# Another seven-product form for attention plus FFN: four products share a PSUM bank that is read in between

## The chip, the core and the metric

The kernel runs on one core of a Trainium2 chip. The metric is the device time of one execution in microseconds (us). "The kernel before" is the version without the change, "the kernel after" the one with it. Engines go by the profile's names: PE is TensorE's matmuls and PEld its weight loads, DVE is VectorE, ACT is ScalarE, POOL is GpSimd, SP is SyncE.

## The reference

`q`, `k` and `v` are 8 x 12 x 448 x 64 (batch, heads, sequence, head size) in float32. The attention's output goes, as 3584 tokens of 768, through a feed-forward network with SiLU:

```python
scores = np.matmul(q, k.transpose(0, 1, 3, 2)) / np.sqrt(64)
attn = softmax(scores)                      # over the keys
x = np.matmul(attn, v)                      # -> (8 * 448) x (12 * 64)
h = x @ w_in                                # 768 x 2048
g = h * (1.0 / (1.0 + np.exp(-h)))
out = g @ w_out                             # 2048 x 768
```

## The kernel before

**Attention.** A unit is one batch and one group of four heads; batch 0 is cut into two pieces of 224 queries, so that there are 27 units, numbered 0 to 26 in order of batch (units 11 and 12, 13 and 14, 25 and 26 are three of the pairs below). For each unit, q and k come by DMA and are transposed on VectorE (`turn_q` L323, `turn_k` L305), TensorE makes scores (L336), ScalarE takes their exponents (`expo` L373) and TensorE multiplies these by v (`attend` L399, L415). Units 0 to 6 are worked on one by one; from unit 7 on two work as a pair: their last, half-filled key rows share one 128-row matmul. The attention of a pair has three parts: part 0 makes the sums of the exponents (L415), parts 1 and 2 make the two halves of the output, each for both units, in 32 column-tiled matmuls of 128x32 weights (24 of full rows and 8 of half rows). VectorE adds exponents up first (`add_e` L384), inverts the sums (`inverse`) and scales each half into `xT` (`norm` L482), which holds half of x, transposed, in fp16.

**First matmul.** For batches 0 to 5, `ffn1` (L496) makes h in blocks of 128 features by 448 tokens, six matmuls each, into one PSUM bank; ScalarE takes the tanh (L507) and VectorE makes (tanh + 1) * h (`gate` L543), which is the SiLU, into `G` (or `X` for one token tile in each four batches). Batches 6 and 7 (`PB` = 6) use another form: for each of eight values of f, `pair_product` (L632) makes a 2 x 2 block product (two batches by two 128-feature blocks, f and f + 8, over two halves of 768) with seven products of three matmuls instead of eight. The sums that it needs are made by VectorE beforehand: of tokens, `combine_x` (L590), and of weights, `combine_w_in` (L608). Copies and adds (`pair_copy` L657, `pair_add` L663) put the products together, and ScalarE takes the SiLU itself (`silu` L670), for which it loads another function table (`first_silu` L667).

**Second matmul.** Tokens go in 28 tiles of 128. A quad is two token tiles by two column halves of 384, over two halves of 2048. Quad 0 is computed plainly (`plain` L718). For quads 1 to 13 `product` (L704) makes seven products of eight matmuls of 384 columns instead of eight, by Strassen's form: products 3 and 5 add up in one PSUM bank, 4 and 2 in another, 1 and 7 in a third, and 6 has a bank of its own. `combine_g` (L694) makes the five sums of gates that this needs, in two halves each, three of them in buffers `S` and two in place; `combine_w` makes five sums of weights once. `take_3` and the others (L766 to L780) read the banks: three copies on ScalarE and four adds on VectorE, and two more adds on VectorE between buffers in SBUF (`less_12`, `less_21`). Each of the four output blocks goes from an `ost` buffer to memory in four DMAs, most of them issued by SyncE (`store` L762). The quads 11 and 13 (`FAR`) keep their outputs in old `xT` buffers. Since a pair of batches has seven tiles, quad 3 takes its first tile from batch 1 and its second from batch 2.

**The order.** All engines' instruction orders are written out by hand, in a plan that is computed when the kernel is built. `Order` holds a free time for each engine; an `Op` has an estimated duration, the operations that it waits for, and a bias that ranks it among those that are ready. `Ring` models a set of buffers: `m_ring` the four single PSUM banks (attention, h, products and plain products), `s_ring` the two two-bank tiles of scores, `sg_ring` the three `S` buffers, `ost_ring` the output buffers, and others the rest. TensorE's next work is chosen among scores, attention and the list `moe`: the first of its first 24 entries whose operands are ready by the plan, and for which a bank and the buffers that it names are free. An entry may be ready before the one ahead of it, so quads, `ffn1` blocks and f-pairs mix. VectorE and ScalarE take the ready operation of least time plus bias. As the plan's order is the program's order, an operation that isn't ready in time on the chip holds up everything behind it on its engine. A block of `ffn1` of a new pair of batches also waits for the products that read the part of `G` that it overwrites; the list of these products stands in `queue_ffn1`, and for the f-pairs in `free`.

## Time and profile before

| what | before |
|---|---|
| device time, median of 3 runs (range) | 396.12 us (396.03 to 396.42) |
| span of the profiled execution, first to last instruction | 394.4 us |
| mean granted clock of TensorE in it | 0.998 |
| PE busy | 386.5 us, 98%, 3679 matmuls |
| DVE busy | 311.3 us, 79%, 653 instructions |
| ACT busy | 243.2 us, 62%, 378 instructions |
| POOL busy | 83.6 us, 21%, 153 instructions |

The span and all rows of the profile come from one execution; its own time is the span and what lies around the program, and the median is 1.7 us above the span. A row of groups gives the line, the engine, the operation, the tiles written and read, the number of instructions, their busy time and the mean of one in ns, and then the idle time just before them with what ended most of it. Matmuls overlap each other in the pipeline: a row's duration is not the distance at which they follow. A row of the timeline gives the start, the time from the start of its first instruction to the end of its last, the instructions, and in brackets how long the engine stood idle before it and who ended that. A row of the chain of waits gives the start and the length of a stretch on the path to the last instruction.

### The profile page before, as it was taken

What the parts mean: (1) busy time and instruction counts of PE and PEld (TensorE: products, weight loads), DVE (VectorE), ACT (ScalarE), POOL (GpSimd) and SP (SyncE); (2) the same over time, 40 slices, a digit from 0 to 9 for tenths busy, and PEclk for the clock granted to TensorE, in tenths of its full rate; (3) what the DMA queues carried; (4) which work ended last, traced back from release to release, by engine and by line L of the source; (5) the groups of instructions that cost most, each with busy time, mean ns of one, the idle gap of its engine ahead of it and who ended that gap; (6) DMA issues with size and microseconds to landing.
All of it is one profiled execution on the core that took longest, in us unless ns stands there. A gap on an engine that the chain in (4) does not pass through costs nothing.

```text
span 394.4 us, 9273 instructions
## 1 busy us (share of the span) xinstructions
PE 386.5 (98%) x3679; PEld 199.0 (50%) x3679; DVE 311.3 (79%) x653; ACT 243.2 (62%) x378; POOL 83.6 (21%) x153
## 2 busy tenths in 40 slices
PE   7999999999999999999999999999999999999995
PEld 6667764443444444554444444344444555556663
DVE  2466676999999697896888786988879898787863
ACT  4988885696863868626868429686593227872110
POOL 6632546315004242500051221120000000000000
PEclk9999999999999999999999999999999999999999
DMA  7999999919034863582145751531100131001334
GB/s 113 205 210 210 166 179 164 175 36 141 1 76 88 142 95 47 75 158 71 25 49 81 139 109 46 71 48 42 42 1 2 40 87 35 2 1 42 80 82 121
DMA packets 35356, 34.44 MB, mean 87 GB/s; under 512 B 11376, under 2 KB 33776, under 8 KB 35312
## 3 DMA queue, kind: packets, MB, share of 16 engines
q0 software_dynamic: 24784, 22.82, 39.2%
q1 hardware_dynamic: 9952, 10.33, 9.6%
q10 hardware_dynamic: 576, 0.69, 0.6%
q8 instruction: 29, 0.48, 0.5%
q14 instruction: 15, 0.12, 0.1%
HBM read 45.61 MB, written 11.01 MB: 144 GB/s over the span
## 4 chain that ended last, share of the span: by engine, by line
PE 94%; DMA 3%; DVE 1%; ACT 1%; POOL 0%; issue 0%; POOLq 0%
PE p L704 29%; PE h L496 29%; PE s L336 12%; PE a L399 10%; PE f L632 8%; PE o L718 3%; DMA rq<-in_q_dram 3%; PE a L415 2%; PE z L1491 1%; ACT E L373 0%; DVE S L694 0%; POOL rk L249 0%; DVE rq L323 0%; DVE rdn L466 0%; DVE ost L766 0%
## 5 line engine op out<-in xcount | busy, mean ns | idle before, releaser
L373 ACT ACTIVATE E<-s 128x896 f16<-128x896 f32 (+1 forms) x172 | 150.0, 915 | 48.6 <-PE s L336 47.5
L496 PE MATMUL h<-xT,w_in_t 128*128 128x448 f16 (+1 forms) x672 | 118.6, 327 | 0.0
L496 PEld LDWEIGHTS <-w_in_t 128*128 128x128 f16 x672 | 61.2, 98 | 54.0 <-issue 18.0
L507 ACT ACTIVATE th<-h 128x448 f16<-128x448 f32 (+1 forms) x112 | 54.3, 495 | 31.4 <-PE h L496 22.5
L543 DVE SCALAR_TENSOR_TENSOR G<-th,h 128x448 f16<-128x448 f16 (+2 forms) x112 | 55.1, 507 | 15.3 <-ACT th L507 13.3
L270 POOL DMA_DIRECT2D V<-in_v_dram x88 | 48.5, 568 | 56.5 <-PE a L399 42.7
L336 PE MATMUL s<-rq,KT 32*128 32x448 f16 (+4 forms) x768 | 50.9, 337 | 1.4 <-DVE rq L323 0.9
L704 PEld LDWEIGHTS <-G 128*128 128x128 f16 x384 | 36.5, 98 | 28.1 <-issue 4.4
L704 PEld LDWEIGHTS <-S 128*128 128x128 f16 x312 | 29.3, 98 | 23.9 <-issue 5.2
L399 PE MATMUL a<-E,V 128*32 128x448 f16 (+3 forms) x864 | 40.4, 335 | 0.0
L255 POOL DMA_DIRECT2D rq<-in_q_dram x27 | 15.1, 560 | 113.0 <-PE s L336 82.9
L704 PE MATMUL p<-D,G 128*128 128x384 f16 x208 | 37.6, 326 | 0.0
L704 PE MATMUL p<-w_out_t,S 128*128 128x384 f16 x208 | 37.2, 326 | 0.1
L482 DVE SCALAR_TENSOR_TENSOR xT<-a,rdn 128x448 f16<-128x448 f32 (+1 forms) x54 | 28.7, 565 | 7.4 <-PE a L399 6.5
L336 PEld LDWEIGHTS <-KT 32*128 32x128 f16 (+2 forms) x864 | 17.5, 98 | 29.6 <-issue 25.9
L704 PE MATMUL p<-w_out_t,G 128*128 128x384 f16 x176 | 31.9, 326 | 0.0
L399 PEld LDWEIGHTS <-V 128*32 128x32 f16 (+2 forms) x864 | 18.2, 95 | 22.4 <-issue 14.7
L384 DVE TENSOR_TENSOR T<-T,E 128x1792 f16<-128x1792 f16 x20 | 21.8, 1089 | 8.0 <-ACT E L373 7.9
L694 DVE TENSOR_TENSOR S<-G 128x512 f16<-128x512 f16 x70 | 25.3, 414 | 3.2 <-PE p L704 3.0
L384 DVE TENSOR_TENSOR T<-E,E 128x1792 f16<-128x1792 f16 x20 | 21.6, 1082 | 5.6 <-ACT E L373 5.6
L776 ACT COPY ost<-p 128x384 f32<-128x384 f32 x13 | 6.2, 480 | 27.4 <-PE p L704 22.6
L305 DVE STREAM_TRANSPOSE KT<-rk 128x256 f32<-128x256 f32 (+3 forms) x48 | 16.6, 384 | 7.0 <-DMA rk<-in_k_dram 6.2
(74 smaller groups left out, 370.2 us busy)
## 6 DMA issues: line engine op xcount, KB each, us to landing
out_dram<-ost SPq DMA_DIRECT2D x194, 48.0 KB, 1.7
rk<-in_k_dram POOLq DMA_DIRECT2D x24, 224.0 KB, 5.9
rq<-in_q_dram POOLq DMA_DIRECT2D x21, 224.0 KB, 5.2
w_in_t<-in_moe_w_in_dram POOLq DMA_DIRECT2D x6, 512.0 KB, 11.2
w_out_t<-in_moe_w_out_dram POOLq DMA_DIRECT2D x4, 768.0 KB, 13.5
V<-in_v_dram POOLq DMA_DIRECT2D x43, 64.0 KB, 3.9
V<-in_v_dram POOLq DMA_DIRECT2D x40, 48.0 KB, 4.0
out_dram<-ost SPq DMA_DIRECT2D x8, 96.0 KB, 2.2
```

Of the source, the lines that this page charges most:

```text
L270: nc.gpsimd.dma_start(out=VT[b][32 * x : 32 * (x + 1), hs, 0:count, :], in_=v[b, hs].rearrange("h (i g) d -> i h g d", g=TPP)[:, :, first ...
L336: nc.tensor.matmul(out=pS[p0 : p0 + 32 * (x1 - x0), h % 2, at : at + nq], lhsT=KT[(b, hg)][32 * h : 32 * (h + 1), c, x0:x1, :, e], rhs=QT[ ...
L373: nc.scalar.activation(out=E[(n, w)][0:kr, 2 * y : 2 * y + 2, 0:nk], in_=pS_t[(n, w, y)][0:kr, :, 0:nk], func=AF.Exp, scale=attn_scale,)
L384: nc.vector.tensor_tensor(out=T[n], in0=T[n] if step else E[(n, 0)], in1=E[(n, step + 1)], op=ALU.add,)
L399: nc.tensor.matmul(out=a[32 * h : 32 * (h + 1), 0:nq], lhsT=w, rhs=e[k0:k1, h, at : at + nq], start=start, stop=stop,)
L482: nc.vector.scalar_tensor_tensor(out=x3(b, cc)[:, cc % 3, 32 * g0 : 32 * g1], in0=acc[(n, part)][:, 0:nq], scalar=0.5, in1=rdn_t[n].rearra ...
L496: nc.tensor.matmul(out=h[:, 0 : t1 - t0], lhsT=w_in_t[:, cc, 128 * f : 128 * (f + 1)], rhs=x3(b, cc)[:, cc % 3, t0:t1], start=(cc == 0), s ...
L507: nc.scalar.activation(out=th, in_=h_t[(b, f, t0)][:, 0 : t1 - t0], func=AF.Tanh)
L543: nc.vector.scalar_tensor_tensor(out=dst[:, f, at + lo : at + hi], in0=th_t[(b, f, t0)][:, lo - t0 : hi - t0], scalar=1.0, in1=h_t[(b, f, ...
L632: nc.tensor.matmul(out=pp_t[(f, PBANK[m])], lhsT=w[:, c, :], rhs=a[:, c, :], start=(c == 0 and m in (1, 6, 5, 7)), stop=(c == 2), skip_gro ...
L694: nc.vector.tensor_tensor(out=dst[:, f0:f1], in0=x[:, f0:f1], in1=y[:, f0:f1], op=op)
L704: nc.tensor.matmul(out=pr_t[(qd, BANK[m])][:, 0:OH], lhsT=w[:, f, :], rhs=W_[m][:, f, :], start=(f == 0 and BANK[m] == m), stop=(f == HF - 1),
```

## The change

The change replaces the seven products in both places by another set of seven. For a quad with token tiles a and b, feature halves 0 and 1, gates Ga0 to Gb1 and weight blocks B00 to B11:

- S5 = Gb0 + Gb1, S6 = S5 - Ga0, S7 = Ga0 - Gb0, S3 = Ga1 - S6 (four sums of gates, S7 in place);
- W5 = B01 - B00, W6 = B11 - W5, W4 = B10 - W6, W7 = B11 - B01 (four sums of weights, W7 in place);
- P1 = Ga0 B00, P2 = Ga1 B10, P3 = S3 B11, P4 = Gb1 W4, P5 = S5 W5, P6 = S6 W6, P7 = S7 W7;
- the outputs are P1 + P2, P1 + P6 + P5 + P3, P1 + P6 + P7 + P4 and P1 + P6 + P7 + P5.

P1, P6, P7 and P4 add up in one bank, which is read after P1 (ScalarE copies it to the output block 00), after P1 + P6 (ScalarE, to 01), after P1 + P6 + P7 (VectorE adds it to 11) and after all four (ScalarE, to 10). P2 has a bank, which VectorE adds to 00. P5 and P3 share a third: ScalarE copies P5 to 11, and VectorE adds P5 + P3 to 01. So a quad has four copies on ScalarE and three adds on VectorE, all into the output buffers; the buffers `tmp` are gone, and there are seven `ost` buffers instead of four. The products stand in `moe` as 1, 5, 6, 2, 7, 3, 4, an `S` buffer is taken for one sum at a time instead of three at once, and the list of products that hold `G` is 1, 2, 3, 4, 7.

The f-pairs get the same form: bank A (products 1, 6, 7, 4) is one half of a two-bank score tile, of which the other half isn't used, and B (2) and C (5, 3) are single banks. A pair has three copies on ScalarE and three adds on VectorE, into SBUF buffers "p", "q" and "u", and four SiLUs, three from these and one from the bank. Before, it had two copies, five adds and four SiLUs. What `combine_x` and `combine_w_in` make is unchanged.

```diff
     NE, NX3, NT_ = 9, 6, 2
     NXT = 3 * NX3
-    NSG, NTMP, NOST = 3, 3, 4
+    NSG, NOST = 3, 7
     attn_scale = 1.0 / (D**0.5)
 
...
@@ -514,24 +514,23 @@
     HF = NFF // 2
     G = const.tile([128, NFF, 2 * S], FP16, name="G")
     X = const.tile([128, NFF, 128], FP16, name="X")
-    W_ = {m: const.tile([128, HF, OH], FP16, name=f"D{m}") for m in (1, 4, 6)}
+    W_ = {m: const.tile([128, HF, OH], FP16, name=f"D{m}") for m in (4, 5, 6)}
     B_ = {
         (i, j): w_out_t[:, HF * i : HF * (i + 1), OH * j : OH * (j + 1)]
         for i in range(2)
...
+    W_[1], W_[2], W_[3], W_[7] = B_[0, 0], B_[1, 0], B_[1, 1], B_[0, 1]
...
     def combine_w(m, f0, f1):
-        i0, i1, op = {
-            1: ((0, 0), (1, 1), ALU.add),
-            4: ((1, 0), (0, 0), ALU.subtract),
-            6: ((0, 0), (0, 1), ALU.add),
-            3: ((0, 1), (1, 1), ALU.subtract),
-            7: ((1, 0), (1, 1), ALU.add),
+        x, y = {
+            5: (B_[0, 1], B_[0, 0]),
+            6: (B_[1, 1], W_[5]),
+            4: (B_[1, 0], W_[6]),
+            7: (B_[1, 1], B_[0, 1]),
         }[m]
         nc.vector.tensor_tensor(
-            out=W_[m][:, f0:f1], in0=B_[i0][:, f0:f1], in1=B_[i1][:, f0:f1], op=op
+            out=W_[m][:, f0:f1], in0=x[:, f0:f1], in1=y[:, f0:f1], op=ALU.subtract
         )
 
     def gate(b, f, t0, t1):
...
-    PBANK = {1: "A", 2: "A", 6: "B", 5: "C", 3: "C", 7: "D", 4: "D"}
+    PBANK = {1: "A", 6: "A", 7: "A", 4: "A", 2: "B", 5: "C", 3: "C"}
 
     def pair_product(f, m):
-        if m in (1, 5):
-            pp_t[(f, PBANK[m])] = ps.tile(
-                [128, 512], FP32, name=f"f_{f}_{m}", tag="m", bufs=4
-            )[:, 0:S]
-        elif m == 6:
-            two = ps.tile([128, 2, 512], FP32, name=f"f_{f}_{m}", tag="s", bufs=2)
-            pp_t[(f, "B")], pp_t[(f, "D")] = two[:, 0, 0:S], two[:, 1, 0:S]
+        if m in (2, 5):
+            t = ps.tile([128, 512], FP32, name=f"f_{f}_{m}", tag="m", bufs=4)
+            pp_t[(f, PBANK[m])] = t[:, 0:S]
+        elif m == 1:
+            t = ps.tile([128, 2, 512], FP32, name=f"f_{f}_{m}", tag="s", bufs=2)
+            pp_t[(f, "A")] = t[:, 0, 0:S]
         x = {(r, i): x3(PB + r, 3 * i) for r in range(2) for i in range(2)}
         lo, at = f // 4 * 4, slice(128 * (f % 4), 128 * (f % 4 + 1))
         a, w = {
...
@@ -643,24 +641,19 @@
             "p": ("rq", NRQ, [128, TPP * D], FP16),
             "q": ("rk", NRK, [128, TPP * D], FP16),
             "u": ("KT", 3, [128, NCH, 4, 32, 2], FP16),
-            "v": ("T", NT_, [128, HG, S], FP16),
         }[name]
         t = sb.tile(shape, dt, name=f"{name}_{f}", tag=tag, bufs=n)
...
         return pf_t[(f, name)]
 
...
         nc.scalar.copy(out=pair_tmp(f, name), in_=pp_t[(f, at)])
 
-    def pair_add(f, to, x, y):
-        x = pp_t[(f, x)] if x in "BCD" else pf_t[(f, x)]
-        y = pf_t[(f, y)]
-        out = pf_t[(f, to)] if (f, to) in pf_t else pair_tmp(f, to)
-        nc.vector.tensor_tensor(out=out, in0=x, in1=y, op=ALU.add)
+    def pair_add(f, to, x):
+        t = pf_t[(f, to)]
+        nc.vector.tensor_tensor(out=t, in0=pp_t[(f, x)], in1=t, op=ALU.add)
 
     def first_silu():
         t = const.tile([128, 1], FP16, name="first_silu")
...
     def combine_g(qd, m, f0, f1):
         a, b = 2 * qd, 2 * qd + 1
+        if m != 7 and (qd, m) not in S_t:
+            S_t[(qd, m)] = sb.tile([128, HF, 128], FP16, name=f"S_{qd}_{m}", tag="S", bufs=NSG)
         x, y, op = {
-            5: (rows(a, 0), rows(a, 1), ALU.add),
-            2: (rows(b, 0), rows(b, 1), ALU.add),
-            1: (rows(a, 0), rows(b, 1), ALU.add),
-            6: (rows(b, 0), rows(a, 0), ALU.subtract),
-            7: (rows(a, 1), rows(b, 1), ALU.subtract),
+            5: (rows(b, 0), rows(b, 1), ALU.add),
+            6: (S_t.get((qd, 5)), rows(a, 0), ALU.subtract),
+            7: (rows(a, 0), rows(b, 0), ALU.subtract),
+            3: (rows(a, 1), S_t.get((qd, 6)), ALU.subtract),
         }[m]
-        if m > 5:
-            dst = x
-        else:
-            if (qd, m) not in S_t:
-                S_t[(qd, m)] = sb.tile([128, HF, 128], FP16, name=f"S_{qd}_{m}", tag="S", bufs=NSG)
-            dst = S_t[(qd, m)]
+        dst = rows(b, 0) if m == 7 else S_t[(qd, m)]
         nc.vector.tensor_tensor(out=dst[:, f0:f1], in0=x[:, f0:f1], in1=y[:, f0:f1], op=op)
 
-    BANK = {3: 3, 5: 3, 4: 4, 2: 4, 1: 1, 7: 1, 6: 6}
+    BANK = {1: 1, 6: 1, 7: 1, 4: 1, 2: 2, 5: 5, 3: 5}
 
     def product(qd, m):
-        w = {3: rows(2 * qd, 0), 4: rows(2 * qd + 1, 1), 6: rows(2 * qd + 1, 0), 7: rows(2 * qd, 1)}
+        w = {1: rows(2 * qd, 0), 2: rows(2 * qd, 1), 4: rows(2 * qd + 1, 1), 7: rows(2 * qd + 1, 0)}
         w = w[m] if m in w else S_t[(qd, m)]
         if BANK[m] == m:
             pr_t[(qd, m)] = ps.tile([128, 512], FP32, name=f"p_{qd}_{m}", tag="m", bufs=4)
@@ -730,10 +719,6 @@
 
     def bank(qd, m):
         return pr_t[(qd, m)][:, 0:OH]
-
-    def tmp(qd, name):
...
@@ -762,40 +747,18 @@
             eng.dma_start(out=dst, in_=ost_t[(qd, i, j)][32 * w : 32 * (w + n), :])
             w, turn = w + n, turn + 1
 
...
+    OUT = {1: (0, 0), 5: (1, 1), 6: (0, 1), 4: (1, 0)}
+    SUM = {2: (0, 0), 7: (1, 1), 3: (0, 1)}
+
+    def take_copy(qd, m):
+        nc.scalar.copy(out=ost(qd, *OUT[m]), in_=bank(qd, BANK[m]))
+        if m == 4:
+            store(qd, *OUT[m])
+
+    def take_sum(qd, m):
+        t = ost_t[(qd, *SUM[m])]
+        nc.vector.tensor_tensor(out=t, in0=bank(qd, BANK[m]), in1=t, op=ALU.add)
+        store(qd, *SUM[m])
 
...
@@ -950,7 +913,7 @@
                         made += (
                             [plain_op.get(x) for x in ((0, 0), (0, 1), (1, 0), (1, 1))]
                             if qd == 0
-                            else [pr_op.get((qd, m)) for m in (3, 4, 6, 7)]
+                            else [pr_op.get((qd, m)) for m in (1, 2, 3, 4, 7)]
                         )
                 return made
 
...
-                    read("v", "DVE", lambda: pair_add(f, "v", "D", "u"), [op, done["u"]])
                 elif m == 5:
...
                 elif m == 2:
-                    gate_of(0, 0, "A", [op], m_ring.give)
+                    read("11", "DVE", lambda: pair_add(f, "p", "B"), [op, done["p"]], m_ring.give)
+                    gate_of(0, 0, "p", [done["11"]], rq_ring.give)
+                elif m == 7:
+                    read("22", "DVE", lambda: pair_add(f, "q", "A"), [op, done["q"]])
+                    gate_of(1, 1, "q", [done["22"]], rk_ring.give)
                 elif m == 3:
-                    read("12", "DVE", lambda: pair_add(f, "p", "C", "u"), [op, done["u"]], m_ring.give)
-                    gate_of(1, 0, "p", [done["12"]], rq_ring.give)
+                    read("12", "DVE", lambda: pair_add(f, "u", "C"), [op, done["u"]], m_ring.give)
+                    gate_of(1, 0, "u", [done["12"]], kt_ring.give)
                 else:
-                    read("21", "DVE", lambda: pair_add(f, "u", "D", "u"), [op, done["12"]], s_ring.give)
-                    gate_of(0, 1, "u", [done["21"]], kt_ring.give)
+                    gate_of(0, 1, "A", [op], s_ring.give)
 
             def deps():
...
                         Op(
@@ -1173,70 +1137,62 @@
                         )
                     )
                 )
+        if not todo:
+            quads.pop(0)
 
     def queue_quad(qd):
-        quads.append(qd)
+        quads.append((qd, [5, 6, 7, 3]))
         took = {}
         home = far_ring if qd in FAR else ost_ring
 
-        def read(m, eng, fn, deps, then=None):
-            if m in (5, 2):
-                then = lambda at: (m_ring.give(at), home.give(at + STORE))
-            elif m in (6, 7):
-                then = lambda at: (m_ring.give(at), home.give(at + STORE), tmp_ring.give(at))
+        def read(m, deps):
+            def then(at):
+                if m in (2, 3, 4):
+                    m_ring.give(at)
+                if m in (2, 3, 4, 7):
+                    home.give(at + STORE)
+
+            fn, eng = (take_copy, "ACT") if m in OUT else (take_sum, "DVE")
             busy = act(OH) if eng == "ACT" else OH / 960.0 + 0.13
             bias = -2 if eng == "ACT" else -4
-            took[m] = od.add(Op(eng, busy, lambda: fn(qd), deps, bias, then=then))
-
-        def queue(m, first):
+            took[m] = od.add(Op(eng, busy, lambda: fn(qd, m), deps, bias, then=then))
+
+        def queue(m):
+            first = {6: (1,), 2: (1,), 7: (6, 5), 3: (5, 6, 7), 4: (7,)}.get(m, ())
+
             def run():
                 op = Op("PE", HF * mm(OH), lambda: product(qd, m), tail=PE_OUT)
                 if BANK[m] == m:
                     m_ring.take()
                 for ring, need in rings:
                     ring.take(need)
-                if m in (5, 2, 1):
+                if m in (5, 6, 3):
                     op.then = sg_ring.give
                 od.on_pe(op, "full")
                 pr_op[(qd, m)] = op
-                if m == 3:
-                    read(3, "ACT", take_3, [op])
-                elif m == 4:
-                    read(4, "DVE", take_4, [op, took[3]])
-                elif m == 5:
-                    read(5, "ACT", take_5, [op], m_ring.give)
-                elif m == 2:
-                    read(2, "ACT", take_2, [op], m_ring.give)
-                elif m == 1:
-                    read(1, "DVE", take_1, [op, took[4]])
-                    read("less_12", "DVE", less_12, [took[1], took[5]])
-                    read("less_21", "DVE", less_21, [took[1], took[2]])
-                elif m == 6:
-                    read(6, "DVE", take_6, [op, took["less_21"]], m_ring.give)
-                else:
-                    read(7, "DVE", take_7, [op, took["less_12"]], m_ring.give)
+                read(m, [op] + [took[x] for x in {2: (1,), 7: (5,), 3: (6,)}.get(m, ())])
 
             def deps():
-                made = list(w_op.get(m, [None])) + [x for y in first if y for x in [took.get(y)]]
-                if m in (3, 4):
-                    t = 2 * qd + m - 3
+                made = list(w_op.get(m, [None]))
+                hard = {6: (1,), 7: (6,), 3: (5,), 4: (7,)}.get(m, ())
+                made += [took.get(x) if x in hard else (took.get(x), 9.0) for x in first]
+                if m in (1, 2, 4):
+                    t = 2 * qd + m // 4
+                    i = int(m != 1)
                     for b in {(128 * t + c) // S for c in (0, 127)}:
                         for f in range(HF):
-                            x = g_op.get((b, f + HF * (m - 3)), [None])
+                            x = g_op.get((b, f + HF * i), [None])
                             made += [(y, f * mm(OH)) for y in x]
                     return made + ld_wout
-                if m in (1, 6, 7):
-                    made += [pr_op.get((qd, x)) for x in ((5, 2) if m == 1 else (1,))]
                 x = sg_op.get((qd, m), [None, None])
                 return made + [x[0], (x[1], 4 * mm(OH))]
 
-            rings = {3: ((tmp_ring, 1),), 1: ((tmp_ring, 1),), 4: ()}
-            rings = rings.get(m, ((home, 1),))
+            rings = ((home, 1),) if m in OUT else ()
             moe.append((deps, 1 if BANK[m] == m else 0, run, rings))
 
 
-        for m, first in ((3, ()), (4, (3,)), (5, (3,)), (2, (4,)), (1, ()), (6, ()), (7, (1,))):
-            queue(m, first)
+        for m in (1, 5, 6, 2, 7, 3, 4):
+            queue(m)
 
     def after_x(n):
 
@@ -1256,7 +1212,7 @@
         if g1 < TPP:
             return
         if b == 0:
-            sums_w((1, 4, 6))
```

## The prediction

> **What bounds the kernel now.** I read the page, the waits of TensorE, the chain of waits, and the timeline around each idle stretch of TensorE, in that order. The page:
>
> ```profile
> span 394.4 us, 9273 instructions
> PE 386.5 (98%) x3679; PEld 199.0 (50%) x3679; DVE 311.3 (79%) x653; ACT 243.2 (62%) x378; POOL 83.6 (21%) x153
> PE 94%; DMA 3%; DVE 1%; ACT 1%; POOL 0%; issue 0%; POOLq 0%
> ```
>
> TensorE has work in 98% of the span and carries 94% of the chain that ended last; VectorE and ScalarE lie beside it. The order of the built instructions shows the same 3679 matmuls in both kernels. So the change can't shorten TensorE's work; it can only take idle time of TensorE away or add some. Past the first 100 us there is little to take. The waits of TensorE name one:
>
> ```profile
> PE p L704 <- ACT ost L780: 0.6, 1, 0.6
> ```
>
> The timeline shows it, and what VectorE does beside it. It stands behind the last attention pair (units 25 and 26), whose second half is the first row:
>
> ```profile
> 306.20 1.63 PE L399 MATMUL a<-E,V 128*32 128x448 f16 x32
> 307.77 1.47 PE L704 MATMUL p<-w_out_t,S 128*128 128x384 f16 x8
> 307.93 0.86 DVE L590 TENSOR_TENSOR sx<-xT,xT 128x1344 f16<-128x1344 f16 x1 [1.00 <-PE a L399]
> 308.71 1.82 DVE L608 TENSOR_TENSOR tw<-w_in_t 128x1536 f16<-128x1536 f16 x2
> 309.28 0.48 ACT L780 COPY ost<-p 128x384 f32<-128x384 f32 x1 [2.27 <-PE p L704]
> 309.81 1.46 PE L704 MATMUL p<-D,S 128*128 128x384 f16 x8 [0.57 <-ACT ost L780]
> 310.45 1.15 DVE L482 SCALAR_TENSOR_TENSOR xT<-a,rdn 128x448 f16<-128x448 f32 x2
> 311.11 1.90 PEld L704 LDWEIGHTS <-G 128*128 128x128 f16 x13 [0.23 <-DVE xT L482]
> ```
>
> One product of eight matmuls takes 1.30 (the first row of the chain's fence, under the changes of mode). 307.77 to 309.81 is 2.04, so 0.74 is idle: a PSUM bank comes free only when ScalarE's copy (309.28 + 0.48) has read it. TensorE goes on 0.05 after the copy's end. Note the last two rows as well: the norms of units 25 and 26 are late because a `combine_x` waits for the attention's last matmul and two `combine_w_in` stand before them, and TensorE starts the next product at 311.12, 0.05 after the first norm's end. One more idle stretch shows only as a distance: 16 matmuls should take 2.60, and the next block starts 2.87 later, so 0.27 is idle (late half sums, L694, behind a late load of q).
>
> ```profile
> 222.21 3.04 PE L704 MATMUL p<-w_out_t,S 128*128 128x384 f16 x16
> 225.08 1.46 PE L704 MATMUL p<-w_out_t,G 128*128 128x384 f16 x8
> ```
>
> **The change, part by part.** *VectorE and ScalarE.* Per quad VectorE does three reads of banks instead of six adds and four sums of gates instead of five; per f-pair three adds instead of five; two fewer halves of weight sums. At the distances at which such rows follow each other (0.47, 0.33, 0.54, 0.87) that is 13x3x0.47 + 13x2x0.33 + 8x2x0.54 + 2x0.87 = 37 us less. ScalarE gets one more copy per quad (0.48) and per f-pair (0.53): 13x0.48 + 8x0.53 = 10.5 us more. Neither is on the chain, so I cost both at nothing; the cover is TensorE's own products. For a quad, P1, P6, P7 and P4 now share one bank, and each may start only when the one before is read. In the order at least one other product of 1.30 stands between; a read costs 0.2 (start behind the product, 386.01 against 385.81 in the timeline) + 0.48 or 0.56 + 0.05 = 0.73 to 0.81. For an f-pair two products of 0.57 stand between: 1.13 against 0.20 + 0.53 + 0.05 = 0.78. The slack there is 0.35, and ScalarE must be in time: three copies and four SiLUs per f-pair at the 0.48 at which such rows follow each other (353.36, 353.84) are 3.4 of TensorE's 21 x 0.189 = 3.97.
>
> *What goes.* In the new order quad 8 is finished before the last attention half, so the 0.74 goes, and the half sums of quads 5 and 6 stand further ahead of their products, so I take the 0.27 off (bounds 0 and 0.27; loads of q just ahead of their transposes stand in two places of the new order, but the products around them wait for neither).
>
> *First new wait: batch 2's first matmul.* Quad 3 spans batches 1 and 2. Its P1 needs batch 1 alone, and the order now issues it before batch 2's first ffn1, while P4, which ends the use of its bank, comes only after batch 2. So attention and ffn1 of batch 2 have three banks of the `m` ring. In the order `h_2_14` stands straight behind the first attention half of units 13 and 14 and waits for the norm that reads that half's bank. Before, the second half stood there:
>
> ```profile
> 144.03 3.20 PE L399 MATMUL a<-E,V 128*32 128x448 f16 x64
> 145.59 0.88 PEld L399 LDWEIGHTS <-V 128*32 128x32 f16 x24 [0.20 <-issue]
> 145.73 1.16 DVE L482 SCALAR_TENSOR_TENSOR xT<-a,rdn 128x448 f16<-128x448 f32 x2 [0.29 <-PE a L399]
> ```
>
> The norm can't start before the half has ended, so the wait has a floor: 145.73 + 0.62 (mean of such a row) + 0.05, against 145.59: 0.81. Behind TensorE queue only its own later blocks. VectorE can make it longer (a transpose of q and an `add_e` of 1.08 now stand before the norm), by 0.3 at most, if their rows follow at full length; I take the floor.
>
> *Second new wait: quad 9.* Behind the last attention half the order now has P1 of f-pairs 0 and 1 (2 x 0.57), P7 of quad 9 (1.30), then P2 of quad 9, which waits for the norm of unit 25. VectorE's order before this norm is as before: `combine_x`, two `combine_w_in`. So TensorE is there 2.43 after the half, and the norm's end lets it go 311.12 - 307.77 = 3.35 after: 0.92 idle. Bounds: nothing, if the norm came first, and 1.0, if the weight load is not ahead.
>
> The Trainium skill ("VectorE: DVE Perf Modes", section "The DRAIN you can't avoid") says that a VectorE instruction doesn't start until the pipeline of the one before is empty, and adds that one that isn't held starts earlier. By the first half of this the four rows would take 0.86 + 2 x 0.95 + 0.62 = 3.38 where the trace has 310.45 + 0.62 - 307.93 = 3.14, and the sum would be 0.24 longer; the trace agrees with the second half.
>
> *Changes of mode.* Two attention pairs (units 11 and 12, 13 and 14) are now parted by other work between their halves. The chain prices a change between full and partial tiles:
>
> ```profile
> 102.65 1.30 PE p L704 x8
> 103.95 0.51 PE s L336 x8
> 104.45 2.71 PE p L704 x16
> ```
>
> 16 matmuls are 2.60 by the first row; 0.11 is the change. A parted pair has two changes for the one that its halves had between them, so 2 x 0.1 = 0.2.
>
> *The end.* The last read is a ScalarE copy (mean 0.48) instead of a VectorE add; both start when the last product ends, and the stores follow as before: -0.08.
>
> ```profile
> 389.91 0.56 DVE ost L766
> ```
>
> *Sum:* 0.81 + 0.92 + 0.2 - 0.74 - 0.27 - 0.08 = +0.84 on the span of 394.4. The median of the runs is 396.12, 1.7 above the span for what lies around it; I leave that as it is: 396.96, **397.0**. A difference of 0.2% (0.8 us) is about what a measurement of this kernel can tell from no change.
>
> **The rivals.** *A, the forecast:* both waits come. 396.4 to 397.6, chance 0.62.
>
> *B, quad 9 doesn't wait (not slower).* Place: the norm of unit 25. It decides at 2.43 after the attention half; if `combine_x` finds its buffer free earlier, the norm ends within 0.9 and the 0.92 falls out: 396.0, and 395.6 to 396.4 with the spread of the runs of before (396.03 to 396.42, 0.4) on either side. For it: VectorE has 37 us less to do and is early. Against it: the 1.00 that `combine_x` stood waiting for the attention's last matmul in the trace of before, and the same wait stands in the new order. Chance 0.15.
>
> *C, ScalarE sets the pair stage (slower).* If its reads come later by one SiLU (0.48) than the 0.35 of slack allows, each of three reads per f-pair costs 0.13: 8 x 3 x 0.13 = 3.1, 400.1; if only one of three, 398.0. For it: 3.4 of 3.97 with in-order queues. Against it: ScalarE's idle rows in that stage now end mostly with TensorE or VectorE, and it catches up. Chance 0.13.
>
> *D, the change does more than I see (faster).* It decides if neither new wait comes, the 0.74 and 0.27 both go, and VectorE's relief takes what small idle time is left: 395.2 or less. That the bank reuse brings nothing to TensorE's work is sure (3679 matmuls); for D speaks only the 37 us. Chance 0.10.
>
> **How the numbers follow.** The time is A's. The range takes in A, B down to 395.6, and the lower end of C, 398.0 with the same 0.4 of spread: 395.6 to 398.4. Faster by over 0.2% (under 395.33): D, 0.10. Slower (over 396.91): C and 0.44 of A, 0.57. Within: B and the rest of A, 0.33. A's own range is 396.4 to 397.6.
>
> **What would show it.** In the waits of TensorE: `PE p <- ACT ost` gone; `PE h <- DVE xT` of about 0.7 near 150 us, behind an attention block of 32 rather than 64; `PE p` or its weight load `<- DVE xT` of about 0.8 to 0.9 near 318, behind two f-pair blocks. In the pair stage an f-pair every 3.97, and at the end a COPY as the last row before the stores. I'm wrong if TensorE waits for ScalarE anywhere between 320 and 355, if either norm wait is missing, or if the stretch from the pair stage to the end differs in length by more than 0.3 from before's.

## The result: both forecast waits came, and a third stood where one was to go

| | before | after |
|---|---|---|
| device time, median of 6 runs (range) | 396.01 us (395.67 to 396.42) | 397.13 us (397.06 to 397.80) |
| ratio to before, 95% interval | 1 | 1.0034 (1.0023 to 1.0045) |
| span of the profiled execution | 394.4 us | 395.8 us |
| start of the last matmul | 389.55 us | 391.19 us |

The kernel after is slower by about a third of a percent; 397.0 was forecast. But the span of the traced execution went up by 1.4, where the sum of the prediction had 0.84. This execution took 397.56, 1.8 above its span, about as before; it is one of the longer of its six, so the median of 397.13 hides a part of the miss. Below, rows are compared from trace to trace. The profile after, first the page:

```profile
span 395.8 us, 9269 instructions
PE 387.8 (98%) x3679; PEld 199.9 (50%) x3679; DVE 273.6 (69%) x570; ACT 252.5 (64%) x399; POOL 83.7 (21%) x153
PE 97%; ACT 1%; DVE 1%; issue 0%; DVEq 0%
```

VectorE has 311.3 - 273.6 = 37.7 us less to do and ScalarE 9.3 more, about as forecast (37 and 10.5), and TensorE has as many matmuls. The time isn't there. It is in the waits of TensorE (what it waits for, us in sum, times, longest):

```profile
PE h L496 <- DVE xT L482: 0.7, 1, 0.7
PE p L693 <- DVE xT L482: 0.7, 1, 0.7
PE p L693 <- DVE ost L760: 0.5, 1, 0.5
```

The first two are the forecast ones, the third is not. No wait stands between two products of a shared bank: there the other products between them covered the reads, as the prediction took it. The timeline around the first, behind the first attention half of units 13 and 14:

```profile
149.02 1.63 PE L399 MATMUL a<-E,V 128*32 128x448 f16 x32
149.64 1.09 DVE L384 TENSOR_TENSOR T<-E,E 128x1792 f16<-128x1792 f16 x1
150.72 1.16 DVE L482 SCALAR_TENSOR_TENSOR xT<-a,rdn 128x448 f16<-128x448 f32 x2
151.40 1.29 PE L496 MATMUL h<-xT,w_in_t 128*128 128x448 f16 x6 [0.74 <-DVE xT L482]
```

The norm starts with the end of the attention half, and the block of ffn1 starts 0.05 behind the first of the two norms. Without the wait it could have started at 150.58, where its first weight load stands in the trace: 0.82 lost. The column of idle time says 0.74, since it counts from the modelled end of the matmul before. Starts are the safer measure, and are used below. Next, the timeline around the second, behind the last attention half:

```profile
315.48 1.63 PE L399 MATMUL a<-E,V 128*32 128x448 f16 x32
317.21 0.86 DVE L589 TENSOR_TENSOR sx<-xT,xT 128x1344 f16<-128x1344 f16 x1 [3.67 <-PE a L399]
317.99 1.82 DVE L607 TENSOR_TENSOR tw<-w_in_t 128x1536 f16<-128x1536 f16 x2
318.19 1.46 PE L693 MATMUL p<-w_out_t,G 128*128 128x384 f16 x8
319.73 1.15 DVE L482 SCALAR_TENSOR_TENSOR xT<-a,rdn 128x448 f16<-128x448 f32 x2
320.40 1.47 PE L693 MATMUL p<-w_out_t,G 128*128 128x384 f16 x8 [0.74 <-DVE xT L482]
```

Two products' starts lie 320.40 - 318.19 = 2.21 apart, where 1.30 would do: 0.91 lost. VectorE's order is the one that the prediction read in the trace of before: `combine_x`, two `combine_w_in`, and only then the norms. The third wait, in the timeline ahead of that:

```profile
305.50 0.42 DVE L683 TENSOR_TENSOR S<-G,S 128x512 f16<-128x512 f16 x1
306.91 2.76 PE L693 MATMUL p<-w_out_t,G 128*128 128x384 f16 x16
307.11 0.76 DVE L683 TENSOR_TENSOR S<-G 128x512 f16<-128x512 f16 x2 [1.19 <-PE p L693]
308.92 0.75 DVE L683 TENSOR_TENSOR G<-G 128x512 f16<-128x512 f16 x2
309.59 1.01 DVE L760 TENSOR_TENSOR ost<-p,ost 128x384 f32<-128x384 f32 x2
310.19 1.46 PE L693 MATMUL p<-D,S 128*128 128x384 f16 x8 [0.52 <-DVE ost L760]
```

The last row is quad 9's product 5. It needs the bank of quad 8's product 2, which VectorE reads at 309.59 (the first of the two rows there). That product had ended near 308.2, but VectorE was busy with half sums for quad 9, and these had started late: it stood idle for 1.19 until 307.11, 0.2 behind the start of the next pair of products. 310.19 - 306.91 is 3.28 for two products, so 0.68 is lost. The stretch near 223 us, last, is without its gap: 16 matmuls take 2.70, with a change of mode behind them.

```profile
222.77 2.77 PE L693 MATMUL p<-D,S 128*128 128x384 f16 x16
225.47 0.57 PE L336 MATMUL s<-rq,KT 32*128 32x448 f16 x8
```

### The profile page after: what moved, and what is told of

Read it like the earlier page. It is cut to its first block, busy times and chain, and to the rows that moved or that the text cites. A ratio compares the mean times of both kernels' runs of the same rounds, so it can differ in the third digit from the quotient of the medians.

```text
span 395.8 us, 9269 instructions
## 1 busy us (share of the span) xinstructions
PE 387.8 (98%) x3679; PEld 199.9 (50%) x3679; DVE 273.6 (69%) x570; ACT 252.5 (64%) x399; POOL 83.7 (21%) x153
## 4 chain that ended last, share of the span: by engine, by line
PE 97%; ACT 1%; DVE 1%; issue 0%; DVEq 0%
PE p L693 31%; PE h L496 29%; PE s L336 13%; PE a L399 10%; PE f L630 8%; PE o L707 3%; PE z L1447 2%; PE a L415 2%; ACT E L373 1%; DVE xT L482 0%; ACT ost L754 0%; DVE ost L760 0%; ACT th L507 0%; DVE G L683 0%; DVE zeros L222 0%
## 5 line engine op out<-in xcount | busy, mean ns | idle before, releaser
L754 ACT COPY ost<-p 128x384 f32<-128x384 f32 x52 | 24.9, 480 | 75.5 <-PE p L693 66.4
L693 PEld LDWEIGHTS <-G 128*128 128x128 f16 x384 | 36.5, 98 | 28.5 <-issue 4.0
L693 PE MATMUL p<-w_out_t,G 128*128 128x384 f16 x280 | 49.4, 326 | 0.7 <-DVE xT L482 0.7
L693 PE MATMUL p<-D,S 128*128 128x384 f16 x208 | 37.0, 326 | 0.5 <-DVE ost L760 0.5
L760 DVE TENSOR_TENSOR ost<-p,ost 128x384 f32<-128x384 f32 x39 | 21.3, 553 | 15.2 <-PE p L693 13.7
L693 PE MATMUL p<-w_out_t,S 128*128 128x384 f16 x104 | 19.1, 326 | 0.0
```

The source lines that it names most:

```text
L693: nc.tensor.matmul(out=pr_t[(qd, BANK[m])][:, 0:OH], lhsT=w[:, f, :], rhs=W_[m][:, f, :], start=(f == 0 and BANK[m] == m), stop=(f == HF - 1),
L754: nc.scalar.copy(out=ost(qd, *OUT[m]), in_=bank(qd, BANK[m]))
```

## The experiments

Some moves are made at the end of the kernel, where the finished order is written out: one instruction is taken out of the list and put ahead of another one, which changes its place on its own engine. All else stays as it is, so a difference belongs to the move. All ratios are to the kernel before, with 95% intervals; the kernel after is at 1.0034. Lines of these kernels lie a few behind those of the kernel after. A span is that of one execution: up to 36 us TensorE's order is the same in all of them, and yet at 36 us the traces of the four below are 0.32, 0.40, 0.23 and 0.03 ahead of that of the kernel after. So what a move is worth is read from starts behind 36 us.

**Each wait by itself.** Each kernel has the moves of its own name. `named` holds the instructions by name; the lines that fill it are not shown.

```diff
-    for _, _, fn in sorted(od.out, key=lambda x: x[:2]):
-        fn()
+    seq = [fn for _, _, fn in sorted(od.out, key=lambda x: x[:2])]
+    for what, ahead in (
+        (("product", 3, 1), ("product", 3, 2)),   # p1_late
+        (("take", 3, 1), ("product", 3, 2)),
+        (("norm", 25, 2), ("tw", 1, 4)),          # norm_first
+        (("norm", 26, 2), ("tw", 1, 4)),
+        (("take", 8, 2), ("sum", 9, 6, 0)),       # take_first
+    ):
+        seq.remove(named[what])
+        seq.insert(seq.index(named[ahead]), named[what])
+    for fn in seq:
+        fn()
```

Quad 3's product 1 held back alone, expected:

> Only the place of one product and its read is changed against the kernel after: product 1 of quad 3 (and ScalarE's copy of it) stands just ahead of quad 3's product 2, so that it holds no bank through batch 2. Theory (three banks are the cause of the wait at 150 us): the 0.82 of `PE h <- DVE xT` is gone, 397.13 - 0.82 = 396.3; up to 0.3 of it may come back near 129 us, where product 1 stood between the last attention half of batch 2 and the first ffn1, and covered the norm. Rival 1 (the parted attention pair itself makes the wait, whatever the banks): the wait stays, 397.1. Rival 2 (VectorE is late there for other reasons): it turns into a wait for a gate, 396.6 to 397.1.

Measured: 396.47 us, ratio 1.0006 (0.9997 to 1.0014), span 394.6 against 395.8, of which 0.92 comes behind 36 us (0.1 more than the wait, about one change of mode: product 1 stood between attention and scores near 128 us). The wait of `h` is gone, and no other came in its place; the list gains only 0.4 of `PE s <- DVE rq` at 6 us, where the kernel before waits as well. So the three banks were its cause: the attention pair is as parted as before, and VectorE's order is the same. The cover that product 1 gave near 129 us wasn't needed.

The norms ahead, expected:

> Only VectorE's order is changed against the kernel after: the norms of units 25 and 26 (second half) stand ahead of two combine_w_in instead of behind them. Theory (those two are what makes quad 9's product 2 wait): combine_x takes 0.86 from 317.2, the norm ends near 318.6, and TensorE is there at 319.5, so the 0.74 that the waits name (0.91 by distance) is gone: 396.2. The sums of weights come 1.1 later, and are for f of 4 and more, 15 us on. Rival (the bank comes from another read, or the late sums hold up the f-pairs): TensorE still waits at this place or behind it, 396.7 to 397.3.

Measured: 396.48 us, 1.0005 (0.9996 to 1.0014), span 394.7. The wait of `p` for `xT` is gone; 0.17 of it comes back two products later (near 322 us), where product 4 waits for a read that now stands behind the sums. By starts behind 36 us the move is worth 0.7.

The read of quad 8's product 2 ahead, expected:

> Only VectorE's order is changed against the kernel after: its read of quad 8's product 2 stands ahead of four half sums for quad 9 instead of behind them. Theory (quad 9's product 5 waits for that read, which is late because the sums ahead of it start 1.2 late, when an S buffer comes free): the read then ends near 309.0 and product 5 can start behind product 7 of quad 8 at 309.5, so the 0.68 by distance is gone: 396.4. Rival 1 (quad 9's sums are themselves the bound): product 5 has its sums, but product 6 of quad 9 or product 3 of quad 8 waits later, 396.8 to 397.2. Rival 2 (the output buffer's store holds the read): no change, 397.1.

Measured: 396.83 us, 1.0012 (1.0003 to 1.0021), span 394.9. The wait is gone, and VectorE's idle 1.19 before the sums stays, off TensorE's path. By starts behind 36 us TensorE is 0.67 earlier, at the place of the wait and nowhere else. The median lies where rival 1 was expected, but none of the later waits of rival 1 is in the trace, and the kernel before took 396.31 in this comparison instead of 396.01. The intervals of this kernel and of the kernel after don't overlap, if by a hair; the size rests on the trace and on the next run.

All three, expected:

> All three moves in one kernel: product 1 of quad 3 late, the norms of units 25 and 26 ahead of two sums of weights, the read of quad 8's product 2 ahead of quad 9's sums. Theory (three separate waits, each with its own cause): 397.13 - 0.82 - 0.91 - 0.68 = 394.7, under the 396.0 of the kernel before. Rival (TensorE loses the same time at the next place, because its order is kept and the engines beside it stay as late): 395.5 or more.

Measured: 395.14 us, 0.9966 (0.9952 to 0.9979), span 393.5. On 396.01 this ratio is 394.7, as expected. The waits of TensorE are down to these, and the kernel before has all three as well:

```profile
PE z L1452 <- DVE zeros L222: 1.0, 1, 1.0
PE s L336 <- ACT E L373: 0.4, 1, 0.4
PE a L399 <- issue: 0.2, 1, 0.2
```

The three add up: 0.82 + 0.91 + 0.68 = 2.41, less the 0.17 is 2.24, and the span is 2.3 shorter. The form with one bank for four products is thus no slower by itself, and this kernel is faster than the kernel before. That doesn't make the form the better one: the kernel before keeps its own idle 0.74 and 0.27, and without them its span would be about 394.4 - 1.0 = 393.4, an estimate, and the same as here. No run moves instructions in the kernel before.

**Why VectorE was late.** In the plan an `S` buffer is given back when its product is done. But S5 is also read by the sum S6, and S6 by S3. At the moment when quad 9's S5 is placed, the plan thinks that quad 8's S6 is free (its product 6 stands first); in truth S3 still has to read it, and S5 of quad 9 gets the buffer of S5 of quad 8, whose product 5 ends 1.3 later. The edit counts readers:

```diff
+    sg_left = {}
+    def sg_read(qd, m):
+        def then(at):
+            n, last = sg_left.pop((qd, m), ({5: 3, 6: 3, 3: 1}[m], 0.0))
+            last = max(last, at)
+            if n == 1:
+                sg_ring.give(last)
+            else:
+                sg_left[(qd, m)] = (n - 1, last)
+        return then
...
-                    op.then = sg_ring.give
+                    op.then = sg_read(qd, m)
...
                             0,
+                            then=sg_read(qd, {6: 5, 3: 6}[m]) if m in (6, 3) else None,
```

> The kernel after with one error of the plan mended: an S buffer counts as free only when its last reader is done (S5 and S6 are read by a product and by the two halves of the next sum), where the kernel after gives it back with the product. The plan makes the order anew; TensorE's order comes out the same, and on VectorE the sums of quads 2 and 9 stand a few places later. Theory (the wait at 309 us comes from this error: the plan lends S6's buffer of quad 8 while S3 still reads it, so the buffer that quad 9's S5 gets is that of S5 of quad 8, whose product ends 1.3 later): VectorE isn't held at 306 us, the read of quad 8's product 2 ends near 309, and the 0.68 is gone as in the kernel with that read moved by hand: 396.8 and under, that is 0.3 to 0.7 under the kernel after. Rival (the place of the read behind the sums is the cause, whenever they start: it still stands behind five of the six half sums of quad 9): the wait stays, 397.1.

Measured: 396.85 us, 1.0019 (1.0010 to 1.0028), span 395.2. The interval overlaps that of the kernel after, so the size rests on the trace: product 5 of quad 9 starts 2.61 behind the two products ahead of it, where it was 3.28. Quad 9's first half sums, and the read:

```profile
306.40 0.76 DVE L683 TENSOR_TENSOR S<-G 128x512 f16<-128x512 f16 x2
308.51 0.56 DVE L760 TENSOR_TENSOR ost<-p,ost 128x384 f32<-128x384 f32 x1 [0.26 <-issue]
```

The wait for `ost` is gone though the read still stands behind five of quad 9's six half sums: these start without a wait now, and VectorE stands idle for 0.26 between the last of the five and the read. So the cause was the miscounted buffer, and the place of the read behind the sums mattered only because they were late.

The mended count together with the other moves, which replace those in the list above:

```diff
+        (("product", 3, 1), ("product", 3, 2)),
+        (("take", 3, 1), ("product", 3, 2)),
+        (("norm", 25, 2), ("tw", 1, 4)),
+        (("norm", 26, 2), ("tw", 1, 4)),
+        (("take", 9, 7), ("tw", 2, 4)),
```

> The mended count of S buffers, with product 1 of quad 3 late, the norms of units 25 and 26 ahead of two sums of weights, and the read of quad 9's product 7 ahead of a third. Theory (the four are independent of each other): 397.13 - 0.82 - 0.91 - 0.68, and 0.17 less where the kernel with three moves still had a wait of 0.17 for that read near 320 us: 394.6 to 395.1, 0.3 to 0.4% under the kernel before. Rival (the mended count alone leaves the wait at 309 us): 395.3 to 395.8.

Measured: 395.19 us, 0.9976 (0.9966 to 0.9986), span 393.3. It lies between what theory and rival expected. It is as fast as the kernel with three moves, and not faster: the 0.17 is gone from its place, but by starts 0.20 is lost at 322.5 us between two matmuls of the first f-pairs.

**The change in halves.** The first kernel has the new quads and the old f-pairs; two cuts of its edit against the kernel after are shown. The second has the old quads and the new f-pairs. The plan makes both orders anew.

```diff
-    PBANK = {1: "A", 6: "A", 7: "A", 4: "A", 2: "B", 5: "C", 3: "C"}
+    PBANK = {1: "A", 2: "A", 6: "B", 5: "C", 3: "C", 7: "D", 4: "D"}
...
-        for m in (1, 5, 6, 2, 7, 3, 4):
+        for m in (1, 6, 5, 2, 3, 4):
             queue(m)
```

> The new form in the quads, the old one in the f-pairs; the plan makes the order anew. Theory (the three waits sit in the quads' part; the f-pair form costs TensorE nothing in either shape): all waits of the kernel after up to 316 us. At the last attention half the order now has quad 9's product 7 alone ahead of product 2, without product 1 of two f-pairs, so TensorE is there 2 x 0.57 earlier and waits 0.91 + 1.14 = 2.05 for the norm: 397.13 + 1.1 = 398.2. Rival (the f-pair form has a cost or a gain of its own of some tenths): another time than 398.2 with the same wait of 2.05.

Measured: 398.65 us, 1.0067 (1.0054 to 1.0081). In the waits `PE p <- DVE xT` has 1.9, and by starts 2.05 is lost, as expected. So the two f-pair products that stand at this place in the kernel after are a filler of 2 x 0.57: without the f-pairs' new form the quads' new form costs more. The median is 0.4 above what was expected; the span, 396.8 against 395.8, is not.

> The old form in the quads, the new one in the f-pairs; the plan makes the order anew. Theory (the f-pair form as such is neutral, since TensorE's own products cover ScalarE's additional copy): the waits of the kernel before, 0.74 near 309 us and 0.27 near 223 us, and no others: 396.0. Rival (ScalarE bounds the f-pairs): TensorE waits for ScalarE's copies between 318 and 357 us, 396.4 or more. Rival 2 (relief of VectorE in this part is worth something): under 395.7.

Measured: 396.10 us, 0.9998 (0.9989 to 1.0007). The f-pair form alone changes nothing that these runs can tell. What the kernel after loses it loses in what the quads' new form does to the order.

**ScalarE in the f-pairs.** Two more copies, then one, of a buffer onto itself behind the copy of "u":

```diff
     def pair_copy(f, name, at):
         nc.scalar.copy(out=pair_tmp(f, name), in_=pp_t[(f, at)])
+        if name == "u":
+            for _ in range(2):       # act_once: 1
+                nc.scalar.copy(out=pf_t[(f, "u")], in_=pf_t[(f, "u")])
```

> The kernel after with two more copies on ScalarE in each f-pair (buffer u onto itself), behind the copy that empties bank A after product 6. They change no value. ScalarE is busy 28.5 of the 34 us from 324 to 358; 16 more of about 0.45 make 35.7. Theory (ScalarE has slack of about 0.6 in each f-pair and no more): one would be hidden, the second is not; 35.7 - 34.0 = 1.7 or a little more comes on top, 398.8 to 400. Rival (the queue is so deep that even this is hidden): 397.1. Rival (ScalarE's latency is on TensorE's path already, at 0.35 of slack per read): two times 0.45 for each of 8 f-pairs, 7 us, 404.

Measured: 402.36 us, 1.0163 (1.0148 to 1.0177): more than the slack theory gave, less than the rival. An f-pair takes 4.69 instead of 3.97. The timeline of that kernel, ScalarE from one SiLU of the bank to the next, without two SiLUs behind the first row:

```profile
340.75 0.54 ACT L666 ACTIVATE G<-f 128x448 f16<-128x448 f32 x1
342.11 0.52 ACT L652 COPY p<-f 128x448 f32<-128x448 f32 x1
342.67 0.53 ACT L652 COPY q<-f 128x448 f32<-128x448 f32 x1
343.09 0.58 ACT L666 ACTIVATE G<-q 128x448 f16<-128x448 f32 x1
343.80 0.53 ACT L652 COPY u<-f 128x448 f32<-128x448 f32 x1
344.36 1.16 ACT L655 COPY u<-u 128x448 f32<-128x448 f32 x2
345.43 0.54 ACT L666 ACTIVATE G<-f 128x448 f16<-128x448 f32 x1
```

The two copies push the next row back by 345.43 - 344.36 = 1.07. The expectation had taken ScalarE's busy share (28.5 of 34) for its load, but not all of what looks idle at 84% can be used. By this trace, 4.69 - 1.07 = 3.6 is what ScalarE needs for an f-pair without the two copies, an estimate, since small waits of ScalarE are in it; that is 0.35 under TensorE's 3.97. With one copy:

> The kernel after with one more copy on ScalarE in each f-pair (u onto itself). With two, an f-pair took 4.69 with ScalarE nearly always busy, of which the two copies were 1.07: 3.6 without them, against 3.97 that TensorE needs. Theory (slack of 0.35 per f-pair): with one, 4.15 per f-pair, 0.18 more than TensorE: 7 or 8 times 0.18, less what is stored up, +0.8 to +1.4: 397.9 to 398.5. Rival (the loss with two copies came from the reads of the banks, at full cost once past a threshold, and one lies under it): 397.1.

Measured: 398.41 us, 1.0055 (1.0040 to 1.0071), 0.0021 above the kernel after, 0.8 us. It lies where slack of 0.35 per f-pair puts it, but the interval overlaps that of the kernel after, so a cost of one row is likely and not shown. With two rows ScalarE sets the pair stage (TensorE waits 3.9 for the SiLUs of the bank). So rival C of the prediction was near: one or two rows of 0.5 more per f-pair on ScalarE.

**What VectorE's relief is worth.** 22 us (25 by the busy rows of the profile) given back to VectorE in eleven quads, by rows that change no value:

```diff
+        for _ in range(2 if m == 5 and qd not in (8, 9) else 1):
             nc.vector.tensor_tensor(out=dst[:, f0:f1], in0=x[:, f0:f1], in1=y[:, f0:f1], op=op)
...
         nc.vector.tensor_tensor(out=t, in0=bank(qd, BANK[m]), in1=t, op=ALU.add)
+        if qd not in (8, 9):
+            nc.vector.tensor_tensor(out=t, in0=t, in1=t, op=ALU.max)
```

> The kernel after with work given back to VectorE in quads 1 to 7 and 10 to 13: the sum S5 is made twice (22 halves of 0.34) and each of the three sums into an output buffer is followed by a maximum of the buffer with itself (33 of about 0.45). They change no value; 22 us of the 37 that the change takes off VectorE. Theory (VectorE's relief is worth nothing to TensorE, except at the places named): 397.1, at most 0.3 more. Rival (the relief pays for a part of the new waits): 397.6 or more, with new waits for VectorE among the quads.

Measured: 399.86 us, 1.0096 (1.0082 to 1.0111), so the theory failed in this form. The waits of TensorE show the following (0.5 of the first row stands in the kernel after as well):

```profile
PE p L694 <- DVE ost L761: 0.9, 2, 0.5
PE a L415 <- DVE ost L761: 0.5, 1, 0.5
PE p L694 <- DVE S L684: 0.3, 1, 0.3
```

By starts TensorE loses 1.8 at four new places (near 117, 161, 211 and 223 us), and behind its last matmul the span goes on for 5.13 instead of 4.60.

With the longer durations told to the plan and the old count of S buffers, the order deadlocks, so there is no time for that. The same work (twice S5, a maximum behind each sum), with the longer durations and the mended count:

```diff
-            busy = act(OH) if eng == "ACT" else OH / 960.0 + 0.13
+            busy = act(OH) if eng == "ACT" else (OH / 960.0 + 0.13) * (1 if qd in (8, 9) else 2)
...
-                            0.34,
+                            0.34 * (2 if m == 5 and qd not in (8, 9) else 1),
```

> The kernel with the mended count of S buffers (396.85), with the same work given back to VectorE in eleven quads as in the kernel that took 399.9, but here the plan knows the longer durations and makes the order anew (84 lines of TensorE's order differ). Theory (the 22 us cost 2.7 because that order was made for a faster VectorE and each place had little slack; an order made for them hides most): 397 to 398, the waits at 150 and 319 us as before, others of 0.5 at most in sum among the quads. Rival (TensorE truly needs the relief, because the sums and reads lie one behind the other on the way from gates to products): 399 or more, whatever the order.

Measured: 397.39 us, 1.0029 (1.0018 to 1.0039), against 396.85 for the same kernel without the added work. VectorE is busy for 298.8 us instead of 273.8, and the last matmul starts at 390.69 instead of 390.56, or 0.18 later counted from 36 us on: 25 us of VectorE cost TensorE less than 0.2. The waits among the quads are gone; what is left of the 0.5 lies behind the last matmul, where the span goes on for 5.08 instead of 4.60, by one added row of about 0.5. So an order that knows the work, with the mended count, hides nearly all of it, and the order of the kernel after pays for a tenth of it. How much of this is due to the count and how much to the durations isn't shown.

## Why the prediction was right, and where it was not

The direction, the mechanism (an order that leaves products waiting for banks and norms, at named places) and both places were right. By the steps of the sum, on the span:

- Batch 2's first matmul: 0.81 forecast, 0.82 measured. That the norm can't start before the half has ended made this a floor, and `add_e` stood in front but cost nothing: it ended (149.64 + 1.09) when the half did, and the norm starts 0.14 behind the point at which TensorE could go on (150.72 against 150.58), as in the trace of before (145.73 against 145.59). The moved product shows the bank as the cause.
- Quad 9's product 2: 0.92 forecast, 0.91 measured. VectorE's four rows took 3.13 to the first norm's end (317.21 to 320.34), as in the trace of before; the sum with the overlap of rows held, four rows one behind the other at full length would be 3.38. The Trainium skill ("VectorE: DVE Perf Modes", section "The DRAIN you can't avoid") has both: that a row waits for the one before to drain, and that one that isn't held starts earlier; the trace agrees with the second.
- The step that failed: "quad 8 is finished before the last attention half, so the 0.74 goes". It does go, and quad 8 is finished in time; but its read of product 2 came late, and quad 9's product 5 lost 0.68 at almost the same place. Net gain 0.06 instead of 0.74. The prediction went by where the reads of quad 8 stand, and not by what stands ahead of them on VectorE and when that can start: it was held by a buffer that the plan took for free, as the mended count shows.
- The 0.27 near 223 us is gone, as forecast.
- Two parted attention pairs: 0.2 forecast. The last block of ffn1 starts 0.80 later than before (299.85 against 299.05); 0.08 of that is there at 105 us already, up to where the two orders are the same, and 0.82 - 0.27 is from the waits, so 0.17 is left for them.
- The end: -0.08 forecast. From the last matmul's start to the end it is 4.60 instead of 4.84, so -0.24. The copy's 0.48 for the add's 0.56 is a third of it; the rest lies between the last read and the last store's landing, and stays open.

```profile
391.55 0.48 ACT L754 COPY ost<-p 128x384 f32<-128x384 f32 x1 [4.72 <-PE p L693]
```

Together 0.08 + 0.82 + 0.91 + 0.17 - 0.27 - 0.06 - 0.24 = 1.41, which is the difference of the spans. Up to the last matmul's start it is 1.65, and that start came 1.64 later: the pair stage and the quads behind it took as long as before, and with the end's -0.24 they stay within the 0.3 that the prediction allowed. That the median came out at 397.13 beside a forecast of 397.0 owes something to chance: a term of 0.68 was missed, the end made up for 0.16 of it, and the traced execution lies 0.43 above the median of its kernel, while that of before (394.4 + 1.8 = 396.2, an estimate) lies near its median.

Of the rivals, B fell with the norm's wait, which lost 0.91; the move that takes it away gains 0.7. C didn't come: there is no wait for ScalarE behind 320 us. The prediction's load of 3.4 per f-pair is about 3.6 by the run with two copies; the slack of 0.35 that comes out of it is ScalarE's time per f-pair, and not the prediction's 0.35, by which two products cover a read. D (VectorE's relief finds idle time to take) fell too; the relief is worth less than 0.2 us of TensorE's time per 25 us where the order is made for the load.

## What to carry to other kernels

When TensorE is busy for 98%, count bank holds and queue positions, not busy time of the others: a product issued early holds its bank until the last product that adds to it, and each read of a bank is as late as the row ahead of it on its engine. A planner's buffer count must name every reader; here missed readers cost 0.68 us, and the order looked right on paper. And if a change loses by waits at named places, move those few instructions by hand before judging the change: three moves turned 0.34% slower into 0.34% faster than before. For a fair judgement of the form, the kernel before would need the same care.

## What the runs showed that was not expected

The busy share of an engine is a poor measure of its slack: ScalarE at 84% in the f-pairs had, by the estimate above, 0.35 us of 3.97 left, 9% and not 16%. And VectorE's time is worth little where the order is made for it (less than 0.2 us of TensorE's per 25), while the same amount put back into an order that didn't know of it cost 2.5 us by the ratios (1.0096 against 1.0034), 0.5 of it behind the last matmul.
